# The right half of w1's last row group, read early in small pieces

## The chip, the cores and the metric

The kernel runs on one core of a Trainium2 chip. Its time is the device time in microseconds (us) of one execution. One execution is also recorded by the hardware profiler; its span, from the first to the last recorded instruction, is a little shorter than its time.

## What is computed

Two blocks work on the same x (2 rows of 1024) and are mixed by a gate:

```
g = sigmoid(sum(x * gate_w))
a = attention(x @ wq, k_cache, v_cache) @ wo      # 32 heads of 128, 16384 positions, one query a row
h = gelu(layernorm(x) @ w1)                       # 1024 to 1024
hs = shifted(h) @ w2                              # shifts along the sequence
x1 = x + hs
b = x1 + gelu(layernorm(x1) @ w3) @ w4            # 1024 to 3584 to 1024
out = g * a + (1 - g) * b
```

The sequence has length 1, so all that the shifts leave of h is zeros. The kernel still computes h: layernorm(x) @ w1 and its GELU are run to the end, and h2 and the output are built from the shifted zeros. All weights and caches are bfloat16. K and V are 536.9 MB together; the kernel reads 572.5 MB in all.

## The kernel before

**Memory.** Nearly all of what is read goes into one tile, `mem`, with 128 partitions and five cells of `CELL` = 16384 bfloat16 elements a partition. `region(cell, elements, offset)` gives a stretch of it. A unit of K or V (two heads of one batch) is `NJ * Dh` = 32768 elements a partition, which is two cells. `K_CELL = (0, 1)`: K of batch 0 covers cells 0 and 1, K of batch 1 covers cells 1 and 2. V covers cells 3 and 4. wq lies in cells 3 and 4 first, w2 in cell 2, later w3 in cell 3 onward. The two K units share cell 1, so the scores of a unit begin with the half that the next load needs.

**Queues.** SP's queue carries almost every load, in the order of the program: wq, the first K, w3, the second K, the first V, then K and V in turn. ACT's queue carries x and gate_w (`rows`), w2 and, at the end, the output. A DMA that must wait holds all that stands behind it on the queue of its engine. Which waits there are, the framework works out from the tiles that instructions read and write; loads and sums put in a "no dep" group are kept out of that and use semaphores of their own, and a `declare_fence` names the instruction by which later users of the same memory wait.

**The head.** PE multiplies `rows` by a small identity to get x with the model dimension on partitions (`xT`, line 231; row group r of the eight holds the dimensions p * 8 + r). When wq has landed it makes q (`rows4`, line 203). Then follow the gate (lines 275 to 288), the first layer norm (`layernorm_T`, lines 295 to 320), which gives `xn1T`, the w2 layer (`layer`, on `shT`, the zeros that the shifts leave), the second layer norm, the scores of the first K unit (`score_chunks`, a transpose on DVE at line 454 and matmuls at line 460) and the w3 layer.

**The loop.** It runs over pairs of heads, two units (one a batch) a round: scores of one unit, softmax, and the product with V of the unit before (`pv`, line 514).

**The tail.** `TAIL` lists the last loads: wo, w4 in three parts, and w1 in four parts, `hidden0` to `hidden3` (5 row groups, 2, and the left and right half of the last one). `load_tail` issues them at line 588, each with a semaphore of its own. `output` waits for each in turn and adds it up: `add_rows` (line 394) for wo and w4, after which the output is written, and `add_hidden` (line 412) for w1. Its sums are kept in `oacc[0]` (columns 0 to 511) and `oacc[1]` (columns 512 to 1023), each as four groups g of 128 columns on partitions from 32 g on. `hidden_gelu` (line 424, ACT) follows for each half. An `in_order` pass fixes every engine's instructions in the order of the program.

Of the kernel before, what the change touches and what calls it, by code (L numbers as in the profile page):

```python
# [10 lines left out]
FP32 = mybir.dt.float32  # L11
BF16 = mybir.dt.bfloat16
ACTF = mybir.ActivationFunctionType
ALU = mybir.AluOpType
# [9 lines left out]
def kernel(  # L24
# [15 lines left out]
    nc = tc.nc  # L40
    P = nc.NUM_PARTITIONS
    B, Sq, D = A_x.shape
    _, H, Sk, Dh = A_k_cache.shape
# [3 lines left out]
    KC = D // P  # L47
# [11 lines left out]
    Q4 = 4  # L59
    QP = P // Q4  # L60
    CELL = NJ * Dh // 2
    G1 = D // Q4
# [3 lines left out]
    const = ctx.enter_context(tc.tile_pool(name="const", bufs=1))  # L66
# [3 lines left out]
    mlp = ctx.enter_context(tc.tile_pool(name="mlp", bufs=1))  # L70
# [3 lines left out]
    def misc_psum(shape, dtype=FP32):  # L74
        return mps.tile(shape, dtype, tag="misc", name="misc")
# [4 lines left out]
    def region(cell, elements, offset=0):  # L80
        at = cell * CELL + offset
        return mem[:, at : at + elements]

    def load_weight(W, cell, offset=0, pieces=None, queue=nc.sync):
        K, N = W.shape
        dst = region(cell, K // P * N, offset)
        src = W.rearrange("(p r) n -> p (r n)", p=P)
        r = 0
        for n in pieces or (K // P,):
            at = slice(r * N, (r + n) * N)  # L90
            queue.dma_start(out=dst[:, at], in_=src[:, at])
            r += n
        return dst.rearrange("p (r n) -> p r n", n=N)

    wq = load_weight(A_wq, 3)
    rows = const.tile([B + 1, D], BF16, name="rows")
    nc.scalar.dma_start(out=rows[0:B], in_=A_x.rearrange("b s n -> (b s) n"))
    nc.scalar.dma_start(out=rows[B : B + 1], in_=gate_w.unsqueeze(0))
    w2 = load_weight(B_w2, 2, queue=nc.scalar)

    K_CELL = (0, 1)
    V_CELL = 3
# [10 lines left out]
    def load_v(hp, b, cell=V_CELL):  # L113
# [3 lines left out]
    ident_f = const.tile([P, P], FP32)  # L117
# [3 lines left out]
        out=ident_s[:], in0=ident_f[:], scalar1=-scale, scalar2=None, op0=ALU.mult  # L121
# [10 lines left out]
        out=mask4[:], in_=mask4[:], compare_op=ALU.is_ge, fill=0.0,  # L132
# [3 lines left out]
        out=mask4[:], in_=mask4[:], compare_op=ALU.is_ge, fill=0.0,  # L136
# [11 lines left out]
        out=lmat[:].rearrange("p (g h k) -> p g h k", h=2, k=4),  # L148
        in_=hm2[:].unsqueeze(1).unsqueeze(3).to_broadcast([P, P // 8, 2, 4]),
# [5 lines left out]
        out=lane[:],  # L155
        in_=ident_f[:].rearrange("p (c k) -> p k c", k=QP),
        axis=AX.X,
        op=ALU.add,
# [3 lines left out]
    for g in range(Q4):  # L162
        nc.vector.tensor_scalar(
            out=spread[:, g],
            in0=lane[:].unsqueeze(1).to_broadcast([P, Q4, QP]),
# [3 lines left out]
    oacc = [ops.tile([P, 4 * Dh], FP32, name=f"oacc{k}") for k in range(2)]  # L169
# [57 lines left out]
    ident_b = const.tile([B + 1, B + 1], BF16, name="ident_b")  # L227
# [9 lines left out]
    xT = rowsT[:, :, 0:B]  # L237
# [54 lines left out]
    def layernorm_T(src, dst, name):  # L292
        bview = src.rearrange("p c b -> p b c")
        s1 = mlp.tile([P, B], FP32, name=f"{name}_s1")
        nc.vector.tensor_reduce(out=s1[:], in_=bview, axis=AX.X, op=ALU.add)
        t1 = misc_psum([P, B])
        nc.tensor.matmul(t1[:], lhsT=ones_f[:], rhs=s1[:], start=True, stop=True)
        nm = mlp.tile([P, B], FP32, name=f"{name}_nm")
        nc.vector.tensor_scalar(out=nm[:], in0=t1[:], scalar1=-1.0 / D, scalar2=None, op0=ALU.mult)
        cen = mlp.tile([P, KC, B], FP32, name=f"{name}_cen")  # L300
        nc.vector.tensor_tensor(
            out=cen[:], in0=src, in1=nm[:].unsqueeze(1).to_broadcast([P, KC, B]), op=ALU.add
        )
        sq = mlp.tile([P, KC, B], FP32, name=f"{name}_sq")
        nc.vector.tensor_tensor(out=sq[:], in0=cen[:], in1=cen[:], op=ALU.mult)
        s2 = mlp.tile([P, B], FP32, name=f"{name}_s2")
        nc.vector.tensor_reduce(
            out=s2[:], in_=sq[:].rearrange("p c b -> p b c"), axis=AX.X, op=ALU.add
        )
        t2 = misc_psum([P, B])  # L310
        nc.tensor.matmul(t2[:], lhsT=ones_f[:], rhs=s2[:], start=True, stop=True)
        ve = mlp.tile([P, B], FP32, name=f"{name}_ve")
        nc.vector.tensor_scalar(
            out=ve[:], in0=t2[:], scalar1=1.0 / D, scalar2=LN_EPS, op0=ALU.mult, op1=ALU.add
        )
        rstd = mlp.tile([P, B], FP32, name=f"{name}_rstd")
        nc.gpsimd.tensor_tensor(
            out=rstd[:], in0=ve[:], in1=neg_half[:].to_broadcast([P, B]), op=ALU.pow
        )
        nc.vector.tensor_tensor(  # L320
            out=dst, in0=cen[:], in1=rstd[:].unsqueeze(1).to_broadcast([P, KC, B]), op=ALU.mult
        )

    def gelu_T(pre, C):
        sq = mlp.tile([P, C, B], FP32, name=f"gelu_sq{C}")
# [20 lines left out]


    compute_gate()
    layernorm_T(xT, xn1T[:], "ln1")
    nc.vector.memset(shT[:], 0.0)  # L350
    for shift in (1, -1, 2, -2):
        if Sq > abs(shift):
# [49 lines left out]
                tc.declare_no_dep(mm.ins, group=group, reason="tail semaphores")  # L402
        return mm

    GH = G1 // 2

    def add_hidden(first, weight, halves, group):
        rows_at = weight.rearrange("p (r h g c) -> p r h g c", h=len(halves), g=Q4, c=GH)
        for r in range(rows_at.shape[1]):
            for k, half in enumerate(halves):  # L410
                for g in range(Q4):
                    mm = nc.tensor.matmul(  # L412
                        oacc[half][QP * g : QP * g + B, 0:GH],
                        lhsT=xn1T[:, first + r, :],
                        rhs=rows_at[:, r, k, g, :],
                        start=(first + r == 0),
                        stop=(first + r == KC - 1),
                        skip_group_check=True,
                    )
                    tc.declare_no_dep(mm.ins, group=group, reason="tail semaphores")  # L420
        tc.declare_fence(mm.ins, group=group)

    def hidden_gelu(half):
        gelu = nc.scalar.activation(  # L424
            out=h_rows[:, half * GH : (half + 1) * GH],
            in_=oacc[half][:, 0:GH],
            func=ACTF.Gelu_apprx_tanh,
        )
        tc.no_tile_sem_insts.add(gelu.ins.name)
        tc.add_to_no_dep_group("stored", gelu.ins)  # L430
# [114 lines left out]
    def turn_heads():  # L545
        apart = mlp.tile([P, B, H, Q4], BF16, name="apart")
        for b in range(B):
            nc.vector.tensor_tensor(
                out=apart[:, b],
                in0=o_all[:, b].unsqueeze(2).to_broadcast([P, H, Q4]),  # L550
                in1=mask4[:].unsqueeze(1).to_broadcast([P, H, Q4]),
                op=ALU.mult,
            )
        ps = misc_psum([P, B, QP])
        for b in range(B):
            nc.tensor.matmul(
                ps[:, b], lhsT=apart[:, b].rearrange("p h c -> p (h c)"), rhs=lane_b[:],
                start=True, stop=True,
            )
        t = mlp.tile([P, QP, B], BF16, name="o_turned")  # L560
        nc.vector.tensor_copy(out=t[:], in_=ps[:].rearrange("p b r -> p r b"))
        return t
# [12 lines left out]
        ("hidden0", 1, 0, w1_rows, 0, 5),  # L575
        ("hidden1", 1, 5, w1_rows, 5, 2),
        ("hidden2", 1, 7, w1_rows, 7, 0.5),
        ("hidden3", 1, 7.5, w1_rows, 7.5, 0.5),
    )
    tail_sems = [tc.alloc_semaphore(f"tail{k}") for k in range(len(TAIL))]  # L580

    def tail_piece(k):
        group, cell, at, src, r, n = TAIL[k]
        return region(cell, int(n * D), int(at * D))

    def load_tail(k):
        group, cell, at, src, r, n = TAIL[k]
        dma = nc.sync.dma_start(out=tail_piece(k), in_=src[:, int(r * D) : int((r + n) * D)])
        dma.then_inc(tail_sems[k], 16)
        tc.no_tile_sem_insts.add(dma.ins.name)  # L590
        tc.add_to_no_dep_group(group, dma.ins)
# [72 lines left out]
    def output():  # L664
        mlp_residual()
        o_turned = turn_heads()
        for k, (group, cell, at, src, r, n) in enumerate(TAIL):
            nc.tensor.wait_ge(tail_sems[k], 16)
            if src is wo_rows:
                add_rows(arows, o_turned, 0, tail_piece(k), False, False, group)  # L670
            elif src is w4_rows:
                mm = add_rows(arows, h2T, r, tail_piece(k), False, r + n == FC, group)
                if r + n == FC:
                    tc.declare_fence(mm.ins, group=group)
                    write_out()
            else:
                halves = (0, 1) if n >= 1 else (int(2 * r) % 2,)
                add_hidden(int(r), tail_piece(k), halves, group)
                if len(halves) == 1:
                    hidden_gelu(halves[0])  # L680
        mark = nc.gpsimd.memset(end_mark[:], 0.0)
        tc.declare_fence(mark.ins, group="stored")
        nc.gpsimd.wait_ge(stored, 16)
# [62 lines left out]
```

## Time and profile before

| | us |
|---|---|
| median of 3 runs | 1329.22 (1329.01 to 1329.25) |
| profiled execution, time | 1329.21 |
| profiled execution, span | 1327.4 |
| PE busy | 755.5 (57% of the span) |
| DVE busy | 648.2 (49%) |
| ACT busy | 132.0 (10%) |
| moved by DMA | 572.69 MB, 431 GB/s over the span |

In the profile's lines PE is TensorE's matmul, PEld its weight load, DVE VectorE, ACT ScalarE, POOL GpSimd, and SPq or ACTq a DMA issue on SP's or ACT's queue. L203 is line 203 of the kernel. A row of the timeline gives start, duration, engine, line, operation, what it writes and reads, shapes, the count of merged instructions, and in brackets the idle time of the engine before it and what ended that. The granted clock is the share of TensorE's full clock that it was given.

### The profile page before, as it was taken

How to read it: one execution, taken by the hardware profiler on the slowest of the kernel's cores; microseconds unless marked ns; L12 is line 12 of the kernel's file. 1: busy time of each engine (PE TensorE's matmuls, PEld its weight loads, DVE VectorE, ACT ScalarE, POOL GpSimd, SP SyncE). 2: the span in 40 equal slices, each digit the busy share in tenths (PEclk: the TensorE clock that was granted, in tenths of full speed). 3: DMA queues.
4: the chain of work that ended last, by engine and by line, in shares of the span. 5: the costliest groups of instructions: out<-in, count | busy, mean ns of one | idle time of the engine just before them, and what ended most of it. 6: DMA issues, size and time to landing. Idle time of an engine off the chain costs nothing.

```text
span 1327.4 us, 13019 instructions
## 1 busy us (share of the span) xinstructions
PE 755.5 (57%) x4980; PEld 329.8 (25%) x4980; DVE 648.2 (49%) x507; ACT 132.0 (10%) x206; POOL 11.9 (1%) x48
## 2 busy tenths in 40 slices
PE   1555566655556665555666555566655556665554
PEld 0222222222222222222222222222222222222222
DVE  1654445554444555444455544445554444555410
ACT  0011111001111101111110111111011111101110
POOL 0000000000000000000000000000000000000000
PEclk9777888877778877777887777788777778877776
DMA  9999999999999999999999999999999999999998
GB/s 411 441 437 419 433 440 431 429 436 442 423 432 440 432 429 434 442 425 431 440 440 421 434 442 427 429 440 440 425 431 442 429 431 436 442 423 431 442 429 375
DMA packets 10820, 572.69 MB, mean 431 GB/s; under 512 B 1205, under 2 KB 1461, under 8 KB 1722
## 3 DMA queue, kind: packets, MB, share of 16 engines
q1 hardware_dynamic: 10656, 570.43, 99.4%
q10 hardware_dynamic: 154, 2.11, 0.4%
q8 instruction: 8, 0.13, 0.0%
q14 instruction: 2, 0.02, 0.0%
HBM read 572.53 MB, written 0.00 MB: 431 GB/s over the span
## 4 chain that ended last, share of the span: by engine, by line
DMA 47%; PE 9%; DVE 8%; issue 6%; PEld 1%; DVEq 0%; ACT 0%; SPq 0%; PEldq 0%; ACTq 0%
DMA mem<-in_A_k_cache_dram 42%; PE S L460 8%; DVE KT L454 8%; DMA mem<-in_B_w_dram 3%; DMA mem<-in_A_v_cache_dram 2%; PE oacc L514 1%; PEld L460 0%; PE oacc L412 0%; DVEq L454 0%; PEld misc L532 0%; ACT osb L527 0%; PEld misc L507 0%; SPq L109 0%; ACT h_rows L424 0%; PEld misc L491 0%
## 5 line engine op out<-in xcount | busy, mean ns | idle before, releaser
L460 PE MATMUL S<-KT,qw 128*128 128x512 bf16 x2048 | 546.3, 416 | 356.9 <-DVE KT L454 356.7
L454 DVE STREAM_TRANSPOSE KT<-mem 128x2048 f32<-128x2048 f32 x256 | 570.7, 2282 | 262.2 <-DMA mem<-in_A_k_cache_dram 212.7
L460 PEld LDWEIGHTS <-qw 128*128 128x128 bf16 x2048 | 216.0, 105 | 679.1 <-issue 476.3
L514 PE MATMUL oacc<-mem,pt 128*8 128x512 bf16 x2048 | 118.4, 384 | 7.4 <-DMA mem<-in_A_v_cache_dram 7.4
L485 ACT ACTIVATE Dm<-ident_s,m 128x128 f32<-128x128 f32 x32 | 12.9, 402 | 970.7 <-PE oacc L514 943.1
L498 ACT ACTIVATE pt<-St,nb 64x256 bf16<-64x256 f32 x64 | 89.7, 1401 | 60.6 <-DVE nb L496 59.7
L536 DVE TENSOR_SCALAR o_all<-misc,g_rep 128x2 f32 (+1 forms) x32 | 7.0, 219 | 163.5 <-PE misc L532 163.5
L507 PE MATMUL misc<-rs,lmat 128*128 128x1 f32 x64 | 18.8, 363 | 107.9 <-ACT pt L498 61.3
L514 PEld LDWEIGHTS <-pt 128*8 128x8 bf16 x2048 | 47.4, 87 | 75.6 <-issue 23.8
L532 PE MATMUL misc<-lane,osb 128*128 128x2 f32 x256 | 33.6, 253 | 45.3 <-ACT osb L527 45.3
L508 DVE RECIPROCAL rinv<-misc 128x1 f32<-128x1 f32 x32 | 5.4, 168 | 108.5 <-PE misc L507 60.5
L481 DVE STREAM_TRANSPOSE St<-S 128x512 f32<-128x512 f32 x32 | 22.9, 717 | 66.4 <-PE L514 64.4
L532 PEld LDWEIGHTS misc<-lane,osb 128*128 128x128 f32 x256 | 31.3, 192 | 61.0 <-ACT osb L527 31.6
L507 PEld LDWEIGHTS misc<-rs,lmat 128*128 128x128 f32 x64 | 16.1, 312 | 114.4 <-ACT pt L498 65.0
L527 ACT ACTIVATE osb<-oacc,rinv 128x512 f32<-128x512 f32 x32 | 22.0, 687 | 88.4 <-PE oacc L514 88.4
L498 ACT ACTIVATION_READ_ACCUMULATOR pt<-St,nb 64x1 f32 x64 | 30.5, 477 | 0.0
L381 POOL TENSOR_TENSOR qw<-qdu,mask 128x16 bf16<-128x16 bf16 x32 | 7.3, 261 | 1137.9 <-PEq L705 1075.7
L496 DVE TENSOR_REDUCE nb<-misc 64x1 f32<-64x64 f32 x64 | 14.2, 222 | 6.3 <-PE misc L491 3.8
L491 PE MATMUL misc<-Dm,ones_f 128*128 128x128 f32 x64 | 15.9, 332 | 0.0
L213 DVE STREAM_TRANSPOSE turn<-wide 128x512 f32<-128x512 f32 (+2 forms) x4 | 3.0, 746 | 25.5 <-ACT wide L245 20.5
L203 PE MATMUL oacc<-mem,rowsT 128*2 128x512 bf16 x64 | 5.0, 479 | 16.1 <-DMA mem<-in_A_wq_dram 16.1
L483 DVE TENSOR_REDUCE m<-St 128x1 f32<-128x256 f32 x32 | 13.4, 420 | 1.1
(98 smaller groups left out, 87.8 us busy)
## 6 DMA issues: line engine op xcount, KB each, us to landing
mem<-in_B_w_dram SPq DMA_DIRECT2D x1, 7168.0 KB, 33.6
mem<-in_B_w_dram SPq DMA_DIRECT2D x1, 4096.0 KB, 42.0
mem<-in_B_w_dram SPq DMA_DIRECT2D x1, 2304.0 KB, 32.2
mem<-in_B_w_dram ACTq DMA_DIRECT2D x1, 2048.0 KB, 32.8
mem<-in_B_w_dram SPq DMA_DIRECT2D x1, 1280.0 KB, 34.6
mem<-in_B_w_dram SPq DMA_DIRECT2D x1, 768.0 KB, 33.5
mem<-in_A_k_cache_dram SPq DMA_DIRECT2D x32, 27.8
mem<-in_A_v_cache_dram SPq DMA_DIRECT2D x32, 32.4
```

The costliest lines, as they stand in the source:

```text
L454: nc.vector.transpose(out=kt[:], in_=Kc.rearrange("p j d -> p (j d)").bitcast(FP32))
L460: nc.tensor.matmul(S, lhsT=qw[b][:, v, NG - 1 - m : NG - 1 - m + P], rhs=ktb[:, half * GT : (half + 1) * GT, w, :, e], start=(first and n ...
L481: nc.vector.transpose(out=st[:].rearrange("p j r -> p (j r)"), in_=S[:])
L483: nc.vector.tensor_reduce(out=m[:], in_=st[:, :, 0:NG], axis=AX.XY, op=ALU.max)
L485: nc.scalar.activation(out=Dm[:], in_=ident_s[:], func=ACTF.Copy, scale=m[:, 0:1])
L491: nc.tensor.matmul(R_ps[:], lhsT=ones_f[:], rhs=Dm[:], start=True, stop=True)
L496: nc.vector.tensor_reduce(out=nb[rows], in_=R_ps[rows, rows], axis=AX.X, op=ALU.min)
L498: nc.scalar.activation(out=pts[b][rows, :, e, :].rearrange("p (m a) k -> p a k m", a=GT // 4), in_=st[rows, :, 0:NG].rearrange("p (a k) m ...
L507: nc.tensor.matmul(tot_ps[:], lhsT=lmat[:], rhs=rs[:], start=True, stop=True)
L514: nc.tensor.matmul(oacc[b][QP * q : QP * q + 8, :], lhsT=pts[b][:, g].rearrange("p h k -> p (h k)"), rhs=V[:, 4 * g : 4 * g + 4, :].rearra ...
L527: nc.scalar.activation(out=osb[:], in_=oacc[b][:], func=ACTF.Copy, scale=rinvs[b][:, 0:1])
L532: nc.tensor.matmul(ot[:], lhsT=osb[:, k * Dh : (k + 1) * Dh], rhs=lane[:, k : k + 5 : 4], start=(k == 0), stop=(k == 3),)
```

## The change

The right half of w1's last row group (128 rows of 512 elements, 1 KB each, 128 KB in all) is no longer the last load of the tail. It is read at the head, on SP's queue, between wq and the first K load, into `region(1, ...)`, the start of cell 1, on partitions 0 to 19. It takes eight transfers. The 128 rows are cut into four runs of 20 and four runs of 12; a run is a slot of 512 elements in the free dimension. Transfer k (0 to 3) of the first set carries rows k, k + 4, k + 8, k + 12 and k + 16 of each run of 20, which are five partitions 4 apart; the second set does the same with three rows of each run of 12.

`hidden_few` runs right after the first layer norm: x for these rows is transposed again into the new arrangement (8 matmuls), normalised with the mean and deviation that `layernorm_T` now returns, and multiplied by the pieces in eight matmuls of 512 columns into `oacc[0]`, two PSUM rows, after a wait for the pieces' semaphore. ACT copies the sums to `h_few`. In the tail `hidden_begin` puts them back into `oacc[1]` by four float32 matmuls with an identity, before the wait for wo, and `add_hidden` adds to them. The fourth w1 load is gone; the right half's GELU follows `hidden1`, the left half's `hidden2`.

```diff
+    STEP = 4
+    HW = D // 2
+    GH = G1 // 2
+    FEW = ((5 * STEP, 4), (3 * STEP, 4))
+    SLOTS = sum(n for _, n in FEW)
+    FEW_P = FEW[0][0]
+    w1_right = B_w1.rearrange("(p r) n -> p r n", p=P)[:, KC - 1, HW:D]
+    w1_few = region(1, SLOTS * HW)[0:FEW_P].rearrange("p (s n) -> p s n", n=HW)
...
+    for width, n in FEW:
+        at = len(few_slots)
+        src = w1_right[row : row + width * n].rearrange("(s p) n -> p s n", p=width)
+        for k in range(STEP):
+            few_pieces.append((w1_few[k:width:STEP, at : at + n], src[k:width:STEP]))
...
+    for dst, src in few_pieces:
+        dma = nc.sync.dma_start(out=dst, in_=src)
+        dma.then_inc(few_sem, 16)
+        tc.no_tile_sem_insts.add(dma.ins.name)
+        tc.add_to_no_dep_group("few", dma.ins)
...
-    layernorm_T(xT, xn1T[:], "ln1")
+    nm1, rstd1 = layernorm_T(xT, xn1T[:], "ln1")
+
+    def hidden_few():
+        last_rows = rows[:].rearrange("b (p r) -> b r p", r=KC)[:, KC - 1]
+        shape = [FEW_P, SLOTS, B]
+        ps = misc_psum(shape)
+        x_few = mlp.tile(shape, BF16, name="x_few")
+        nc.vector.memset(x_few[:], 0.0)
+        for s, (first, n) in enumerate(few_slots):
+            nc.tensor.matmul(
+                ps[0:n, s], lhsT=last_rows[:, first : first + n], rhs=ident_b[:, 0:B],
+                start=True, stop=True,
+            )
...
+        nc.tensor.wait_ge(few_sem, 16 * len(few_pieces))
+        for s, (first, n) in enumerate(few_slots):
+            mm = nc.tensor.matmul(
+                oacc[0][0:B, 0:HW],
+                lhsT=xn[0:n, s, :],
+                rhs=w1_few[0:n, s, :],
+                start=(s == 0),
+                stop=(s == SLOTS - 1),
+            )
+            tc.declare_no_dep(mm.ins, group="few", reason="own semaphore")
+        tc.declare_fence(mm.ins, group="few")
+        saved = const.tile([B, HW], FP32, name="h_few")
+        nc.scalar.activation(out=saved[:], in_=oacc[0][0:B, 0:HW], func=ACTF.Copy)
+        return saved
+
+    h_few = hidden_few()
...
+    def hidden_begin():
+        for g in range(Q4):
+            nc.tensor.matmul(
+                oacc[1][QP * g : QP * g + B, 0:GH],
+                lhsT=ident_f[0:B, 0:B],
+                rhs=h_few[:, g * GH : (g + 1) * GH],
+                start=True,
+                stop=False,
+                skip_group_check=True,
+            )
...
-        ("hidden3", 1, 7.5, w1_rows, 7.5, 0.5),
...
+        hidden_begin()
...
-                halves = (0, 1) if n >= 1 else (int(2 * r) % 2,)
-                add_hidden(int(r), tail_piece(k), halves, group)
-                if len(halves) == 1:
-                    hidden_gelu(halves[0])
+                add_hidden(r, tail_piece(k), (0, 1) if n >= 1 else (0,), group)
+                if r + n >= KC - 1:
+                    hidden_gelu(1 if n >= 1 else 0)
```

More of the change, by code (lines that the diff above doesn't have):

```diff
@@ L99 @@
     w2 = load_weight(B_w2, 2, queue=nc.scalar)
+    STEP = 4
[4 more added lines that the diff above has]
+    FEW_P = FEW[0][0]
+    assert sum(k * n for k, n in FEW) == P
+    w1_right = B_w1.rearrange("(p r) n -> p r n", p=P)[:, KC - 1, HW:D]
+    w1_few = region(1, SLOTS * HW)[0:FEW_P].rearrange("p (s n) -> p s n", n=HW)
+    few_sem = tc.alloc_semaphore("few")
+    few_slots, few_pieces = [], []
+    row = 0
+    for width, n in FEW:
[3 more added lines that the diff above has]
+            few_pieces.append((w1_few[k:width:STEP, at : at + n], src[k:width:STEP]))
+        few_slots += [(row + s * width, width) for s in range(n)]
+        row += width * n
+    for dst, src in few_pieces:
[3 more added lines that the diff above has]
+        tc.add_to_no_dep_group("few", dma.ins)
     K_CELL = (0, 1)
@@ L322, in layernorm_T @@
         )
+        return nm, rstd
     def gelu_T(pre, C):
@@ L348 @@
     compute_gate()
-    layernorm_T(xT, xn1T[:], "ln1")
+    nm1, rstd1 = layernorm_T(xT, xn1T[:], "ln1")
[10 more added lines that the diff above has]
+            )
+        at = 0
+        for width, n in FEW:
+            nc.vector.tensor_copy(
+                out=x_few[0:width, at : at + n], in_=ps[0:width, at : at + n]
+            )
+            at += n
+        cen = mlp.tile(shape, FP32, name="few_cen")
+        nc.vector.tensor_tensor(
+            out=cen[:], in0=x_few[:], in1=nm1[0:FEW_P].unsqueeze(1).to_broadcast(shape),
+            op=ALU.add,
+        )
+        xn = mlp.tile(shape, BF16, name="few_xn")
+        nc.vector.tensor_tensor(
+            out=xn[:], in0=cen[:], in1=rstd1[0:FEW_P].unsqueeze(1).to_broadcast(shape),
+            op=ALU.mult,
+        )
+        nc.tensor.wait_ge(few_sem, 16 * len(few_pieces))
[6 more added lines that the diff above has]
+                stop=(s == SLOTS - 1),
+            )
+            tc.declare_no_dep(mm.ins, group="few", reason="own semaphore")
[4 more added lines that the diff above has]
+    h_few = hidden_few()
     nc.vector.memset(shT[:], 0.0)
@@ L403, in add_rows @@
         return mm
-    GH = G1 // 2
+    def hidden_begin():
[7 more added lines that the diff above has]
+                skip_group_check=True,
+            )
     def add_hidden(first, weight, halves, group):
@@ L415, in add_hidden @@
                         rhs=rows_at[:, r, k, g, :],
-                        start=(first + r == 0),
-                        stop=(first + r == KC - 1),
+                        start=(first + r == 0 and half == 0),
+                        stop=(first + r == KC - 1 - half),
                         skip_group_check=True,
@@ L583, in tail_piece @@
         group, cell, at, src, r, n = TAIL[k]
-        return region(cell, int(n * D), int(at * D))
+        return region(cell, int(n * D), at * D)
     def load_tail(k):
         group, cell, at, src, r, n = TAIL[k]
-        dma = nc.sync.dma_start(out=tail_piece(k), in_=src[:, int(r * D) : int((r + n) * D)])
+        dma = nc.sync.dma_start(out=tail_piece(k), in_=src[:, r * D : int((r + n) * D)])
         dma.then_inc(tail_sems[k], 16)
```

## The prediction

> **What bounds the kernel now.** I read the page first: its DMA rows, then the chain that ended last.
>
> ```profile
> DMA  9999999999999999999999999999999999999998
> GB/s 411 441 437 419 433 440 431 429 436 442 423 432 440 432 429 434 442 425 431 440 440 421 434 442 427 429 440 440 425 431 442 429 431 436 442 423 431 442 429 375
> DMA packets 10820, 572.69 MB, mean 431 GB/s; under 512 B 1205, under 2 KB 1461, under 8 KB 1722
> ...
> DMA 47%; PE 9%; DVE 8%; issue 6%; PEld 1%; DVEq 0%; ACT 0%; SPq 0%; PEldq 0%; ACTq 0%
> ```
>
> The DMA engines are busy in every slice, and the chain that ended last is mostly DMA. The 38 inner slices average 433 GB/s. At that rate 572.69 MB take 1322.6 us. The DMA row of the last 3.4 us shows when the stream stops, in slices of 0.085 us:
>
> ```profile
> DMA  7373935645655521100000000000000000000000
> ```
>
> It stops 18 to 19 slices after 1324.0, at about 1325.5. So in the whole execution the stream stood still for only 1325.5 - 1322.6 = 2.9 us: 0.8 us before the first issue (below) and 2.1 us from that issue to full flow. There is no idle DMA time later that could take in a new stop: each microsecond in which the stream rests should show in the time.
>
> Then the timeline of the first 60 us, which is where the change puts its loads and sums (start, duration, engine, line):
>
> ```profile
> 0.80 0.38 SPq L91 DMA_DIRECT2D mem<-in_A_wq_dram  x1
> ...
> 1.24 0.42 SPq L109 DMA_DIRECT2D mem<-in_A_k_cache_dram  x1
> ...
> 27.05 4.98 PE L203 MATMUL oacc<-mem,rowsT 128*2 128x512 bf16 x64 [16.08 <-DMA mem<-in_A_wq_dram]
> ...
> 31.86 0.33 SPq L91 DMA_DIRECT2D mem<-in_B_w_dram  x1
> ...
> 37.72 0.56 PE L311 MATMUL misc<-ln_s,ones_f 128*128 128x2 f32 x2 [0.96 <-DVE ln_s L307]
> ...
> 39.30 0.17 DVE L320 TENSOR_TENSOR xn1T<-ln_cen,ln_rstd 128x16 bf16<-128x16 f32 x1 [0.83 <-POOL ln_rstd L317]
> 39.43 0.07 DVE L350 MEMSET shT<- 128x8 uint32 x1
> ...
> 39.55 1.88 PE L203 MATMUL oacc<-mem,shT 128*2 128x256 bf16 x32 [0.96 <-DVE shT L350]
> 41.48 0.38 ACT L221 ACTIVATE wide<-oacc 128x256 f32<-128x256 f32 x1 [5.70 <-PE oacc L203]
> ...
> 48.50 4.50 DVE L454 STREAM_TRANSPOSE KT<-mem 128x2048 f32<-128x2048 f32 x2 [2.48 <-DMA mem<-in_A_k_cache_dram]
> ...
> 58.72 0.33 SPq L109 DMA_DIRECT2D mem<-in_A_k_cache_dram  x1
> ```
>
> The reader is to see two things. The first K load is issued at 1.24, right behind wq and long before wq has landed; it is what the DMA engines work on from 27 to 48 us. And xn1T, the normalised x that any sum with w1 needs, is ready only at 39.47.
>
> **Where the new pieces lie, and what that makes wait.** One K tile has 32768 elements a partition, a cell 16384. K of batch 0 starts in cell 0, so it covers cells 0 and 1. The new rows are put in cell 1, elements 0 to 4095 of partitions 0 to 19: inside the tile that the first K load writes. That load must therefore come after the matmuls that read the rows. The instruction order of the changed program says the same: on SP stand wq, the eight pieces, and then the K load, which now waits for PE's 95th counted matmul, the last of the eight early sums; in the program before it waits for nothing. Behind it on SP stand w3, the second K load and the first V load, so all of them are held too. The DMA engines have wq, w2 (ACT's queue) and the pieces to move, and then nothing.
>
> **When the K load goes out.** Up to 38.3 the path is that of before: wq lands at 27.05, q, gate, layer norm. The eight small transposes follow the second layer-norm matmul (37.72 + 0.56); eight like them at L231 took 0.63 us, so they end near 39 and lie beside the wait for xn1T. After xn1T DVE makes five small steps: memset (0.07, as L350), two casts from PSUM (0.18 each, as L236), an add and a multiply (0.17 each, as L301 and L320). Dependent steps there start 0.20 apart (36.99, 37.20, 37.40 at L301, L305, L307), so the last ends near 40.3 and PE starts the early sums at 40.4 (before: 0.05 after L350's end). Each streams 512 columns, all eight into the same two PSUM rows, hence one after the other. The cost of one:
>
> ```profile
> 38.00:40.00 2.00, 1.03 (x18) 0.58 (x21) 0.35 (x3) 0.00 (x0) 0.71 (x1) 0.50 1.21 524
> 40.00:42.00 2.00, 1.43 (x28) 0.62 (x20) 0.11 (x1) 0.38 (x1) 0.00 (x0) 0.50 1.21 524
> ```
>
> The columns of this table by stretches are the stretch, its length, busy time of PE, PEld, DVE, ACT and POOL, granted clock, DMA share and GB/s. The granted clock is 0.50 there. At it the 32 matmuls of 256 columns at 39.55, four side by side, took 1.88 us, and ACT could start 1.93 us after them: eight steps of 0.213 us and 0.22 us to the reader. For 512 columns that is 0.427 us, so eight sums take 3.41 us + 0.22 us, and SP issues the K load at 40.4 + 3.63 = 44.05. Bounds: at full clock 1.7 us less; at the 479 ns that is the mean length of L203's 512-column matmuls (the page's group), 0.4 us more.
>
> **How long the stream rests.** Before, wq and w2 (8.39 + 2.10 = 10.49 MB, 24.2 us at 433 GB/s) have gone through at 2.9 + 24.2 = 27.1, and K flows on. After, K flows from 44.05 + 2.1 (the same start from rest as at 0.80) = 46.15. The stop is 46.15 - 27.1 = **19.05 us**. The start from rest is between 1.2 us (the first 5 us moved 263 GB/s, which is 1.96 us lost, 0.8 of it before the issue) and 2.5 us; I take 2.1, from the whole run.
>
> The Trainium skill, in "DMA: Bandwidth & Descriptors", section "Anatomy of one DMA", fits a transfer on the GpSimd path as 2.0 us plus its bytes at 436 GB/s. By it the K load would land 21.2 us after its issue, where my rows give 21.5; the sum would be 0.3 us less.
>
> **What the stop hides, and what is late next.** The eight pieces (128 KB in all) run in the stop and cost nothing unless they come later than 40.4. The four matmuls of the added x and the w2 layer come 4.5 us later behind the early sums (44 to 46.3 instead of 39.55 to 41.43), the second layer norm ends near 50.5: hidden, since K lands near 65.5. ACT's copy of the sums is hidden in the same way. SP's eight extra issues (0.33 to 0.42 us each) stand beside wq's 26 us. From K's landing on everything keeps its distances: w3 is queued right behind K, the second K load goes out 10.2 us after K's landing (48.50 to 58.72) and still 6.8 us ahead of w3's end. So the 19 us are carried to the end and no more is added.
>
> **The tail.** The last transfer of 128 KB goes, 0.30 us of stream. But the end is this:
>
> ```profile
> 1324.18 2.12 PE L412 MATMUL oacc<-mem,xn1T 128*2 128x128 bf16 x64 [2.29 <-DMA mem<-in_B_w_dram]
> ...
> 1326.17 0.47 ACT L424 ACTIVATE h_rows<-oacc 128x128 bf16<-128x128 f32 x2 [1.70 <-PE oacc L412]
> ```
>
> PE works without a break from 1324.18 on the larger pieces, which land as before; four of 64 matmuls leave (0.1 us), and one of the two GELUs no longer follows the last matmul (0.23 us). Between 0 and 0.4 us; I take 0.25. Putting the saved sums back is four float32 matmuls of 128 columns, half of the 1.02 us that L434's four of 256 took at 1293.86; there PE then idles 9 us for wo, so nothing.
>
> **Sum.** 1329.21 us for the profiled execution (span 1327.4 and 1.8 around it; the median is 1329.22) + 19.05 - 0.25 = **1348.0 us**.
>
> **Rivals.**
> (a) Not slower: the pieces end up clear of the first K tile, or the wait of the K load is met before wq has landed. It decides at 27 us: if K is issued before that, the stream never rests, and only the tail's -0.25 is left (1329.0), or up to 1.3 us more if the DMA engines that carry the pieces are the late ones. For it only the change's aim speaks; against it the sizes of cells and tile, and the wait in the instruction order. 2%; this is also the case that the change does not do what it says.
> (b) The clock is full in the early sums: 1.7 us less, 1346.3. PE ran 512-column groups 0.43 us apart from 27.05 and was at full clock by 30, so it can rise after some 3 us of steady work; but the granted clock stays 0.50 until past 46. 10%.
> (c) The last DMA engine decides, not the mean flow. K landed at 48.44 (47.2 us after its issue), later than the mean flow's 2.9 + 18.87 MB / 0.433 = 46.5; after, 44.05 + 21.5 = 65.5. If that lateness is lost in the stop, the shift is 17.1 - 0.25: 1346.1. 12%.
> (d) The pieces land late: if each pays a start from rest of 2.1 us in turn, they end at 27.1 + 16.8 = 43.9, the sums start 3.5 us later, 1351.5. Against it: the tail's last loads are used at 1324.18, 1325.4 and 1326.0, much less than 2.1 us apart. 4%. The Trainium skill, "DMA: Bandwidth & Descriptors", section "Rules for kernel authors", says that transfers under 64 KB are mostly overhead and should be joined into one; pieces of 20 and 12 KB are of that kind, and by its rule they would be late in this way. The order of landings in the tail does not agree with it; no run here shows pieces this small.
>
> **How the numbers follow.** The forecast has 72%, and rivals (b), (c) and (d) are slower as well. From the bounds, -1.7 and -0.9 below, +0.4 and +0.4 above, with a little for what the rows do not show: 1346.0 to 1350.3, which takes in (b) and (c) and leaves out (a) and (d). 0.2%, about what a measurement of this kernel can tell from no change, is 2.7 us; all cases but (a) are far beyond it. Of (a)'s 2% I leave a quarter to a gain of that size, which no row here gives.
>
> **What would show it.** Right: the first K issue near 44 on SP, a stretch with no DMA from about 28 to 45, the first K transposes near 65.5, all later steps 19 us later. Wrong: K issued before 27 us, or a stop that the DMA row does not show; a K issue at 42.4 says (b), at 47 or later (d).

## The result and the profile after

The changed kernel takes 1348.19 us (median of 4 runs, 1347.71 to 1348.54) against 1329.17 us for the kernel before: 1.0143 times as long, with a 95% interval of 1.0125 to 1.0161. The forecast was 1348.0 us. The profiled execution took 1348.3 us with a span of 1346.5 us, 19.1 us more than before.

The DMA rows of the page of the changed kernel:

```profile
DMA  7699999999999999999999999999999999999998
GB/s 316 277 439 435 435 433 436 436 434 430 422 436 436 434 430 436 436 434 436 436 434 428 424 436 436 434 430 436 436 434 436 436 434 428 424 436 436 434 430 380
DMA packets 10836, 572.69 MB, mean 425 GB/s; under 512 B 1221, under 2 KB 1477, under 8 KB 1738
```

The bytes are the same. Only the first two of the 40 slices are clearly below those of before: 316 and 277 GB/s instead of 411 and 441. From the third on the engines are as full as they were, so nothing is made good later.

The DMA rows of 26 to 50 us (40 slices of 0.6 us) show the stop whole:

```profile
DMA  9221000000000000000000100000000099000990
GB/s 411 87 96 60 0 0 0 0 0 0 0 0 0 0 0 0 0 0 0 0 0 0 27 0 0 0 0 0 0 0 0 0 1311 437 0 0 0 765 983 0
```

The stream drops after the first slice, moves only 60 to 96 GB/s in the next three and nothing from 28.4 us on. It takes up again in the slice that begins at 45.2 us. The 27 in between is an instruction load, one packet on q8, the page's instruction queue. A packet is counted where it begins, so a slice can show more than the engines move in it, and the next ones zero.

The timeline of the head, with the lines that answer to those of before:

```profile
1.24 6.27 SPq L121 DMA_DIRECT2D mem<-in_B_w_dram  x8
...
27.07 5.63 PE L228 MATMUL oacc<-mem,rowsT 128*2 128x512 bf16 x64 [16.04 <-DMA mem<-in_A_wq_dram]
...
38.40 0.56 PE L336 MATMUL misc<-ln_s,ones_f 128*128 128x2 f32 x2 [0.96 <-DVE ln_s L332]
...
40.73 0.16 DVE L400 TENSOR_TENSOR few_xn<-few_cen,ln_rstd 20x16 bf16<-20x16 f32 x1
...
40.95 2.71 PE L406 MATMUL oacc<-mem,few_xn 20*2 20x512 bf16 x6 [1.65 <-DVE shT L420]
...
43.47 1.06 PE L406 MATMUL oacc<-mem,few_xn 12*2 12x512 bf16 x2
...
44.55 0.34 SPq L134 DMA_DIRECT2D mem<-in_A_k_cache_dram  x1
...
44.94 0.42 SPq L91 DMA_DIRECT2D mem<-in_B_w_dram  x1
...
66.41 4.50 DVE L533 STREAM_TRANSPOSE KT<-mem 128x2048 f32<-128x2048 f32 x2 [15.20 <-DMA mem<-in_A_k_cache_dram]
```

The pieces are issued at 1.24, the early sums (L406) run from 40.95 to about 44.5, and the first K load (L134) goes out at 44.55, 0.02 us after the last of them ends; before, it went out at 1.24. w3 follows it at once. SP's table of waits puts the whole pause in one line (what waited, for what, in total, times, longest):

```profile
SPq L134 <- PE oacc L406: 37.0, 1, 37.0
```

And the tail:

```profile
1343.59 0.73 PE L491 MATMUL oacc<-mem,xn1T 128*2 128x128 bf16 x40 [2.23 <-DMA mem<-in_B_w_dram]
...
1344.84 0.55 PE L491 MATMUL oacc<-mem,xn1T 128*2 128x128 bf16 x20 [0.52 <-DMA mem<-in_B_w_dram]
1345.28 0.45 ACT L503 ACTIVATE h_rows<-oacc 128x128 bf16<-128x128 f32 x2 [1.35 <-PE oacc L491]
```

In this execution PE does wait once more in the tail, 0.52 us at 1344.84 for the second piece of w1, so it does not work through without a break as the prediction had it. Its first 40 matmuls took 0.73 us here at a granted clock of 1.00, where before they took 1.2 us at 0.50, so it caught up with the loads.

### The profile page after: what moved, and what is told of

It is laid out like the page before. It is cut to its first block, busy times and chain, and to the rows that moved or that the text cites. A ratio compares the mean times of both kernels' runs of the same rounds, so it can differ in the third digit from the quotient of the medians.

```text
span 1346.5 us, 13073 instructions
## 1 busy us (share of the span) xinstructions
PE 759.1 (56%) x5000; PEld 330.5 (25%) x5000; DVE 648.0 (48%) x512; ACT 132.7 (10%) x207; POOL 12.2 (1%) x48
```

## Experiments

Three runs test whether the stop is what costs, two more take the small prices apart, and three settle what moving the load is worth without the stop. Ratios are to the kernel before, with their 95% intervals.

**The pieces in a place that the first K load does not write.** The free half of cell 2, behind w2:

```diff
-    w1_few = region(1, SLOTS * HW)[0:FEW_P].rearrange("p (s n) -> p s n", n=HW)
+    w1_few = region(2, SLOTS * HW, KC * D)[0:FEW_P].rearrange("p (s n) -> p s n", n=HW)
```

> The changed kernel with the eight pieces in the free second half of cell 2 (behind w2) instead of cell 1, so that the first K load has nothing to wait for. Theory (the time is the rest of the DMA stream while the first K load waits for the early sums): K is issued near 7.5 us, behind eight issues of 0.8 us each in the trace, long before wq lands at 27; no stop; about 1329.0 us, at most 1330.3 if the DMA engines that carry 32 rows of 46 ns each are the late ones. Rival (the eight small pieces, or the longer chain of the head, cost the time themselves): both are kept, so 1340 us or more.

Measured: 1330.58 us (1329.12 to 1330.87), ratio 1.0008 (0.9999 to 1.0017). The timeline of this run:

```profile
7.55 0.41 SPq L134 DMA_DIRECT2D mem<-in_A_k_cache_dram  x1
...
40.45 2.71 PE L406 MATMUL oacc<-mem,few_xn 20*2 20x512 bf16 x6 [1.64 <-DVE shT L420]
...
50.62 4.50 DVE L533 STREAM_TRANSPOSE KT<-mem 128x2048 f32<-128x2048 f32 x2
```

The eight pieces, the second transposition of x, the eight sums and their return in the tail are all still there, and 17.6 of the 19.0 us are gone. K is issued at 7.55 and lands 40.8 us later, at 48.35; its transposes start at 50.62 without any wait for DMA, behind the longer head. The rival, that the pieces or the longer head cost the time, falls. The median is 0.3 us over the bound in the expectation; what the rest of 1.4 us is made of is taken up below.

**The sums made twice.** The stop should grow by one pass.

```diff
-        for s, (first, n) in enumerate(few_slots):
+        for s, (first, n) in 2 * list(enumerate(few_slots)):
             mm = nc.tensor.matmul(
```

> The changed kernel with the eight early sums made twice, one pass behind the other; pieces in cell 1 as in the change. Theory (the first K load waits for the last early sum, and the stream rests until then): 3.4 us more by eight sums at the granted clock of 0.50, K issued near 48.0, 1351.6 us (1349.9 if the clock is full in the second pass). Rival (the loss is a fixed price of a stream that starts again, or of the pieces): 1348.2 us.

Measured: 1353.28 us (1352.63 to 1353.74), ratio 1.0182 (1.0165 to 1.0199), 5.1 us over the changed kernel where 3.4 were expected. The timeline of this run says where the rest is from:

```profile
27.16 6.32 PE L228 MATMUL oacc<-mem,rowsT 128*2 128x512 bf16 x64 [16.04 <-DMA mem<-in_A_wq_dram]
...
42.13 6.13 PE L406 MATMUL oacc<-mem,few_xn 20*2 20x512 bf16 x14 [1.64 <-DVE shT L420]
...
49.14 0.34 SPq L134 DMA_DIRECT2D mem<-in_A_k_cache_dram  x1
```

K is issued at 49.14, 4.59 us later than in the changed kernel. 3.41 us of it are the second pass (42.13 to 49.14 is 7.01 us, against 3.60 from 40.95 to 44.55); 1.18 us are the head before it, which starts its sums at 42.13 instead of 40.95, because the 64 matmuls with wq took 6.32 us instead of 5.63 and what stands behind them met the lower clock sooner (0.52 granted from 36 to 38 us, where the changed kernel had 1.00). The span is 1351.3 us, 4.8 more.

**The sums made earlier.** x without mean and deviation is transposed and cast before wq lands, and the sums stand right behind q's matmuls:

```diff
+    x_few = const.tile(few_shape, BF16, name="x_few")
...
     for k in range(2):
         rows4(oacc[k], xT, wq, KC, k * 4 * 512, 512, 512)
...
-                lhsT=xn[0:n, s, :],
+                lhsT=x_few[0:n, s, :],
...
+    h_few = hidden_few()
     qdps = misc_psum([P, 2, 2, Q4, 2 * B * NV])
```

> The changed kernel with the early sums made with x as it is, without mean and deviation (so the right half of h lacks the layer norm in its last row group), right behind q's matmuls; x for them is transposed and cast before wq lands; pieces in cell 1. Theory: PE ends q's matmuls at 32.7, eight sums take 1.7 to 3.4 us, K is issued at 34.5 to 36.2 instead of 44.55, and the time falls by as much: 1338.2 to 1339.9 us. Rival (fixed price of the second start, or of the pieces): 1348.2 us.

Measured: 1337.99 us (1337.88 to 1338.36), ratio 1.0067 (1.0051 to 1.0084). Its timeline:

```profile
32.02 1.89 PE L298 MATMUL oacc<-mem,x_few 20*2 20x512 bf16 x8
...
33.93 0.34 SPq L134 DMA_DIRECT2D mem<-in_A_k_cache_dram  x1
```

At a granted clock of 1.00 (from 32 to 34 us) the eight sums take 1.89 us, and K goes out at 33.93. That is earlier than the expectation had it, and the time is 0.2 us under its range. The three kernels with a stop lie on one line of slope 1:

| kernel | first K issue, us | span, us | span less issue, us |
|---|---|---|---|
| sums right behind q | 33.93 | 1336.1 | 1302.2 |
| the change | 44.55 | 1346.5 | 1301.95 |
| sums twice | 49.14 | 1351.3 | 1302.2 |

Between them each microsecond by which the first K load is late is a microsecond of the kernel. The line meets the span of before, 1327.4, at an issue of 25.3 us. The prediction's own numbers, 27.1 less a start of 2.1, give 25.0.

**The tail alone.** The kernel before without its last load, so that the right half of h lacks the last row group:

```diff
-        ("hidden3", 1, 7.5, w1_rows, 7.5, 0.5),
```

> The kernel before without the last 128 KB load: the right half of w1's last row group is left out of h. The tail's gain alone. Theory: 0.25 us less than before (0 to 0.4), since PE works through the larger pieces to the end; rival (the stream's end sets the end): 0.3 us and the last wait, 0.5 us less.

Measured: 1328.93 us (1328.79 to 1329.06) against 1329.13, ratio 0.9998 (0.9989 to 1.0008). The medians are 0.2 us apart, as expected in the tail, but the interval holds no change too. This is the most that moving the load can bring, since here the bytes are not read at all. The trace tells one thing more: the 64 matmuls with wq took 6.33 us here instead of 4.98, and the second K load was issued at 59.43 instead of 58.72. A head that is later by this much costs nothing while the stream runs.

**The same bytes in one transfer.** The kernel before with 128 partitions by 512 elements read into the free half of cell 2, and four early sums with `xn1T`:

```diff
+    w1_early = region(2, HW, KC * D)
+    dma = nc.sync.dma_start(
+        out=w1_early, in_=B_w1.rearrange("(p r) n -> p r n", p=P)[:, KC - 1, HW:D]
+    )
...
+                lhsT=xn1T[:, KC - 1, :],
+                rhs=w1_early[:, g * GH : (g + 1) * GH],
```

> The same 128 KB read between wq and the first K load as one transfer of 128 partitions by 512 elements into the second half of cell 2; four early sums with xn1T as it is, no second transposition of x; put back in the tail. Theory: no stop, and nothing on single DMA engines: 1328.9 us. Rival (a separate small load at the head costs by itself): over 1330.

Measured: 1329.43 us (1329.07 to 1329.77), ratio 1.0002 (0.9993 to 1.0011). No stop and no measurable change, as the theory has it, though the median is 0.5 us over the 1328.9 that it gave. The bytes that leave the tail come into the head of a stream that is full in both places.

**The head of the pieces with the tail of before.** Against pieces_elsewhere:

```diff
+        ("hidden3", 1, 7.5, w1_rows, 7.5, 0.5),
...
-        hidden_begin()
```

> The head of pieces_elsewhere (eight pieces in cell 2, early sums) with the tail of before: the last 128 KB are read again at the end and the early sums are not put back. The head's price in a stream that does not stop. Theory: 128 KB more at 433 GB/s, 1329.5 us, up to 1330.7 if the engines that carry the pieces are the late ones. Rival (the longer head chain costs time by itself): 4 us more, 1333.

Measured: 1331.06 us (1329.33 to 1331.95), ratio 1.0013 (1.0004 to 1.0022). This is 0.4 us above the bound in the expectation. The head of the pieces costs 1.9 us in a running stream, 0.3 us of it for the 128 KB that are read a second time; the longer head does not cost 4 us. With the tail of the change it is 1330.58, so the tail gives back 0.5 here.

**Eight transfers on all partitions.** The transfer of one_transfer cut into eight:

```diff
+    for k in range(8):
+        at = slice(16 * k, 16 * k + 16)
+        dma = nc.sync.dma_start(out=w1_early[at], in_=w1_right[at])
```

> one_transfer with its 128 KB cut into eight transfers of 16 partitions by 512 elements each; sums as there. Tells the number of small transfers apart from their sitting on few DMA engines and from the longer head, which pieces_elsewhere has besides (1330.58 against 1329.43). If it is the partitions 4 apart (few DMA engines) or the longer head: 1329.4, as one_transfer. If it is eight issues and eight completions: near 1330.6.

Measured: 1330.01 us (1329.7 to 1330.23), ratio 1.0006 (0.9997 to 1.0015). It lies between the two cases: by the medians 0.6 of the 1.15 us that part pieces_elsewhere from one_transfer are the number of transfers. The split is loose: four of the eleven times of pieces_elsewhere are 1329.77 or less, level with one_transfer. The other 0.6 us stay open between the few DMA engines and the longer head; the next run was to tell these apart.

**One transfer with a longer head.** Against one_transfer:

```diff
-        for g in range(Q4):
+        for g in 32 * list(range(Q4)):
```

> one_transfer with its four early sums made 32 times over (32 groups of 0.107 us at the granted clock of 0.50, 3.4 us), so that the head is as late as in pieces_elsewhere, whose first K transposes start at 50.62 instead of 48.5. If the longer head costs time in a stream that does not stop: near 1330.6. If it is hidden, as the prediction had it: 1329.4.

Measured: 1333.4 us (1330.67 to 1334.13), ratio 1.0024 (1.0015 to 1.0034), worse than either case. The timeline shows that the head became longer than meant:

```profile
39.48 3.58 PE L366 MATMUL oacc<-mem,xn1T 128*2 128x128 bf16 x128 [1.26 <-DVE shT L380]
...
46.83 1.65 PE L214 MATMUL oacc<-mem,shT 128*2 128x256 bf16 x25 [3.09 <-issue]
...
52.98 4.50 DVE L493 STREAM_TRANSPOSE KT<-mem 128x2048 f32<-128x2048 f32 x2
...
63.88 0.33 SPq L120 DMA_DIRECT2D mem<-in_A_k_cache_dram  x1
```

The sums take the 3.6 us that were meant. Then PE sits 3.09 us with nothing to wait for but its own instructions, in the middle of a row of equal matmuls. The first transposes start at 52.98 instead of 48.69, and the second K load is issued at 63.88 instead of 59.95. The DMA row of 60 to 72 us of this run (40 slices of 0.3 us) shows what follows:

```profile
DMA  0004999000080000995000070099900000999000
```

Again a packet is counted where it begins, so single zeros say little. w3's last packets (57 KB, an estimated 2.1 us each at a sixteenth of 433 GB/s) begin up to 62.1, two of them at 63.3; nothing is queued behind them until 63.88, and the first packets of the second K come only in the slices from 64.8 on. The queue had run dry, and the stream stopped a second time. Not all of the difference is this stop. The times fall into two groups, four from 1330.67 to 1331.10 and six from 1333.40 to 1334.13, and the trace is one of the second. This profiled execution and that of one_transfer are 4.5 us apart (spans 1332.2 and 1327.7). The sums with wo start 3.0 us later than with one_transfer (1307.46 against 1304.48) and those with the second part of w4 2.9 us later; the other 1.6 us arise in the tail, where w4's third part is used 3.4 us after the second instead of 1.9. Why it comes late there is open. So this run does not tell the few DMA engines from the longer head. It tells something else: how little cover the second K load has.

## Why the prediction was right, step by step

- **The wait.** The first K load waits for the last early sum: 44.55 against 44.5 for the sums' end; SP's 37.0 us of waiting on that one line. Moving the pieces alone removed it. Shown.
- **When the sums start.** Forecast 40.4, measured 40.95. The step of five small DVE operations took less than reckoned (from the end of `xn1T` at 40.17 to PE's start at 40.95, 0.78 us for my 0.93). What was late is what I had left unchanged: the 64 matmuls with wq took 5.63 us instead of 4.98, so the layer norm's second matmul stood at 38.40 instead of 37.72.
- **The sums.** Forecast 3.41 + 0.22 us at the clock of 0.50, measured 40.95 to 44.55 = 3.60, with 0.50 granted from 38 to 46. Rival (b) falls; the 1.89 us of the early version are what it would have needed.
- **The start from rest.** Forecast 2.1 us and 21.5 from K's issue to its landing; measured 44.55 to 66.35, 21.8 us. The 2.1 us themselves were a little too much: the span grew by 19.1 and the tail gave back about 0.2, so by the forecast's own sum the stop was 19.3 us and the full flow began at 46.4, 1.9 us after the issue. The first packets come 0.95 us after it, at 45.50.
- **No slack later.** The slope of 1 over 15.2 us of issue time shows it, down to 0.2 us.
- **Mean flow, not last landing.** K landed 17.9 us later than before (66.35 against 48.44), yet the span grew by 19.1. Rival (c), at 17.1 less the tail, falls: the lateness of the last DMA engine at 48.44 was not carried to the end as such. The three kernels with a stop say the same: K landed 23.1, 21.8 and 21.6 us after its issue, and the span less the issue is 1302.2, 1301.95 and 1302.2.
- **The pieces.** They were through long before PE asked for them: the stream had run out by 28.4, PE started the sums at 40.95 and had last waited for DVE there. Their eight issues took 6.27 us, 0.78 us each and not 0.33 to 0.42, which stood beside wq's transfer and cost nothing. Rival (d) falls, and with it the reading of the Trainium skill's rule on small transfers by which they would be late. As a price in a running stream the rule ("DMA: Bandwidth & Descriptors", section "Rules for kernel authors") has something: eight transfers took 0.6 us more than one by the medians (1330.01 against 1329.43), far from 2.1 us each.
- **The tail.** Forecast 0.25 us, measured 0.2 by the run without the last load, where the interval holds no change too.
- **Rival (a)** gave the price of the change without the stop, 1329.0 or up to 1.3 us more. Pieces clear of the first K tile took 1330.58, 0.3 us above the upper end: the small costs were there, and I had set them too low.
- **A step that held, but with less room than it claimed.** I let the second K load be covered by 6.8 us, counted to the landing of w3's last part. The longer head shows that the cover ends sooner: there the issue came 3.9 us later than with one transfer, still 2.0 us ahead of w3's landing at 65.9, and the stream stopped. There all but two of w3's last packets had begun by 62.1, which puts their end near 64.2 by the estimate above, and the load needed 0.9 us from its issue to its first packets (63.88 to 64.8). In the changed kernel the distance was kept (76.88, 10.5 us after K's landing), so the sum was not touched.

Sum of the steps: the start of the sums 0.55 late, the sums 0.03 short, so K's issue is 0.5 us later than forecast, and the span less the issue is as forecast within 0.3 us: 1348.0 forecast, 1348.19 measured. The mechanism is the one that was forecast; that the total is right to 0.2 us is partly luck, since the late start and the shorter start from rest go against each other.

None of the versions beats the kernel before. The run that does not read the last piece at all is 0.2 us faster by its median, within its interval; no place for the load can bring more.

## What to carry to other kernels

Before a load is put ahead of others on a queue, look up which later load writes the same memory, and what the early data's last reader has to wait for: a buffer that is free in the tail can lie in the middle of the first big tile. In this kernel, whose DMA engines never rest, a load that was moved as one transfer changed nothing measurable, but a held queue cost all the time that the engines stood still. That is not the whole wait: K was held for 37.0 us, and 19 of them cost time, because wq and w2 kept the engines at work up to 27. From there on the time from the held issue to the end was the same within 0.3 us in three kernels. Moving the buffer alone told the stop from the other prices (small pieces, extra sums, a longer head); what is left between these is not told apart.

## What was not expected of the hardware

- The same 64 matmuls with wq took between 4.93 and 6.36 us in the ten profiled executions: groups of 512 columns stand 0.43 us apart for the first 2.8 us (one_transfer) to 5.5 us (sums_twice), then come twice as fast. The kernel before and the one without the last load have the same program up to the tail, and they took 4.98 and 6.33 us. The Trainium skill, "TensorE: Matmul & The Clock Gate", Part 1, says that the window of 3.4 us by which busy time is judged runs freely, so that the rise varies by 0.5 us to either side. The rows agree that the moment varies from run to run; the spread is larger here, 2.7 us. That this is the clock is inferred from the spacing alone, which elsewhere goes with a granted clock of 0.50 (the early sums, 0.43 us for 512 columns): the granted clock of these rows is 1.00 from 24 us on, also over the slow groups.
- With 124 more matmuls and as many weight loads on PE came a pause of 3.09 us in the middle of equal matmuls, with no wait but "issue" (43.7 to 46.8 us). An instruction load begins in it, between 44.5 and 44.75; the kernel before has one between 44.0 and 44.5 and no such pause. That the loading of instructions is the cause was not tried.
